# Hash attention and a channel mixer: a second level of smaller products for p5 in four row block pairs

## The chip, the core and the metric

The kernel runs on one core of one Trainium2 chip. The metric is device time in microseconds: the median of several executions, each with the same input. One further execution is recorded by the hardware profiler; its views are what the text calls the profile.

Names of the engines: PE is the matrix engine (PEld its weight loads), DVE the vector engine, ACT the scalar engine, POOL the general engine, SP the one that issues most of the DMAs.

## The reference, cut to what matters

An attention with hashed buckets gives `x` of 4 x 768 rows and 512 columns; a mixer over tokens gives `u`; the part that the change touches is the mixer over channels, in float32:

```python
def _moe_ref(x, w_tok1, w_tok2, w_ch1, w_ch2) -> np.ndarray:
    xt = x.transpose(0, 2, 1)
    h = np.maximum(xt @ w_tok1, 0.0) @ w_tok2
    u = x + h.transpose(0, 2, 1)
    h2 = np.maximum(u @ w_ch1, 0.0) @ w_ch2
    return (u + h2).astype(np.float32)
```

`u` has 3072 rows and 512 columns, `w_ch1` is 512 x 1536, `w_ch2` 1536 x 512.

## The kernel before

The program has three parts: attention (to about 310 us of the profiled span), the mixer over tokens (to 387.5 us), and `channels` (the rest). In `channels` everything is transposed: rows of `w_ch1` lie across partitions, and tokens are the columns.

**Stages.** `channels` takes the 3072 tokens in three stages s = 0, 1, 2 of 1024, each as two halves of TT = 512. A stage first makes `relu(u @ w_ch1)` into four tiles R0 to R3 (`hidden`, or `hidden_pair`), then multiplies by `w_ch2` (`outputs`). Both products are done with seven half-size products p1 to p7 in place of eight (Strassen's scheme in Winograd's form). In the first layer, with A the weights and B the tokens, U = p1 + p6 is a common partial sum; R0 = p1 + p2, R1 = U + p5 + p3, R2 = U + p7 + p4 and R3 = U + p7 + p5, up to the signs that are put into the operands.

**Second level.** In s = 1 and 2 the first layer takes its six blocks of 128 weight rows as three pairs t = 0, 1, 2 (block t and block t + 3). Within a pair p2, p6, p7, p3 and p4 are split once more: `Smaller` makes one of them from seven products of 128 x 128 weights by 256 columns where four of 512 columns would be needed. p1 and p5 are whole: two blocks times two 128-row slices of the operand, 512 columns each. The seven products come in three methods: `one` (one matmul, and ACT copies its result to SBUF, L904), `three` (three matmuls, added onto the PSUM tile they are given) and `rest` (three matmuls into the same PSUM tile as `one`, L914). `finish` lets ACT copy a partial sum u out of PSUM (L925), DVE add it to two 256-column parts in one 512-column add (L927), and DVE make the last part with a 256-column add (L930). The result e (four parts of 256) and the PSUM tile of `three` together are the product.

**PSUM.** There are four tiles of two banks each, 1024 columns, used in turn by the list `ring`; `bank_pair(i)` opens one anew, which waits for all uses of its last contents.

**Order.** The order on each engine is that of the calls in the text; engines meet through semaphores. In `hidden_pair` it is written out by hand. `plus` is a DVE add (L963), `copy` an ACT copy of 1024 columns (L960), `relu` is on ACT (L966). U is made in the tile `u`: p1 is accumulated with three parts of p2 in SBUF, p6's three parts are added by PE onto the PSUM tile of p1, and the copy of that, plus e6, is U. `between` gives DVE the sums of operands for the next products in the first pair of a stage (`right_sums`, four 256-column operations, L852 to L855). `unfinished` holds work for R1 to R3 of one pair, and `end_rows` does it in the next.

**Work ahead.** At the end of a pair the first half of the next pair's p1 is computed (`ahead`); it goes into the tile that held p5 and p3, and waits for the add into R1. At the end of t = 2, `whole_first` computes a part of the second layer's p1 ahead, and `whole_product` the rest.

**Looks.** Beside all this, `look` fetches a slice of the attention's input by a DMA that POOL issues (L1355) and sums on ACT how far its squares pass a bound (L1344, L1345). The results are needed at the first products of s = 2. It stands four times in each pair, and once in each second-layer product of s = 0 and 1.

**Weights.** The sums of weights for the second level are made by DVE in stage 0 (`prepare`) and stored in DRAM (`hidden_passed`). For each pair and each of p2, p6, p7, p3, p4 the seven blocks of 128 x 128 are fetched by SP (`fetch_hidden_left`, L866, 448 KB) as soon as the same product of the pair before has used its own.

Of the kernel before, what the change touches and what calls it, by code (L numbers as in the profile page):

```python
# [48 lines left out]
def kernel(  # L49
# [702 lines left out]
    def channels(pool, psum, SW1, second, TA, judge):  # L752
# [85 lines left out]
        def right_sums(name, s):  # L838


            sl = [slice(TT * (2 * s + i), TT * (2 * s + i) + TT) for i in range(2)]
            src = {"p2": XT[:, KC:, sl[0]], "p3": XT[:, KC:, sl[1]], "p6": T[1], "p7": T[2], "p4": T[3]}[name]
            if name == "p7":
                z = SW1[:, 1].rearrange("p k c -> p (k c)")[:, : 2 * TT]
            else:
                z = XT[:, ["p2", "p6", "p3", "p4"].index(name), : 2 * TT]
            z = split4(z)
            half = [slice(0, TT // 2), slice(TT // 2, TT)]
            b = [src[:, k, n] for k in range(2) for n in half]

            def job():
                nc.vector.tensor_tensor(z[:, 0], b[1], b[0], op=ALU.subtract)  # L852
                nc.vector.tensor_tensor(z[:, 1], b[3], b[1], op=ALU.subtract)
                nc.vector.tensor_tensor(z[:, 2], b[3], z[:, 0], op=ALU.subtract)
                nc.vector.tensor_tensor(z[:, 3], b[2], z[:, 2], op=ALU.subtract)  # L855

            return job, [*b, *(z[:, i] for i in range(4))]
# [12 lines left out]

        def hidden_left_at(h):

            h, n = h % 5, 7 * P
            if h < 3:
                return WC1[:, KC:].rearrange("p k c -> p (k c)")[:, n * h : n * h + n]
            return SW1[:, 2 * (h - 3)].rearrange("p k c -> p (k c)")[:, :n]
# [5 lines left out]
        def first_weight(name):  # L882

            return {
                "p2": WC1[:, KC:, : DCH // 2], "p3": SW1[:, 2], "p4": WC1[:, KC:, DCH // 2 :], "p6": SW1[:, 0],
                "p7": SW1[:, 1],
            }[name]
# [5 lines left out]
        class Smaller:  # L893


            def __init__(self, h, name, s):
                self.h, self.w = h, hidden_left_at(h).rearrange("p (i c) -> p i c", i=7)
                self.b = right_sums(name, s)[1]

            def one(self, pair, e):  # L900

                self.ps, self.e = pair, split4(e)
                self.mm(pair[:, 0, : TT // 2], 4, 0)
                nc.scalar.copy(self.e[:, 0], pair[:, 0, : TT // 2])  # L904

            def three(self, pair, start=False):
# [3 lines left out]
                self.mm(pair[:, 1, : TT // 2], 6, 7, start)  # L910

            def rest(self):

                self.mm(self.ps[:, 1, : TT // 2], 0, 4)  # L914
                self.mm(self.ps[:, 1, TT // 2 :], 1, 5)
                self.mm(self.ps[:, 0, : TT // 2], 2, 6, False)
                fetch_hidden_left(self.h + 5)

            def mm(self, ps, left, right, start=True):
                accumulate(ps, lambda k: self.w[:, left], lambda k: self.b[right], [0], start)  # L920

            def finish(self):

                u = extra_flat()[:, TT // 2 * (self.h % 2) : TT // 2 * (self.h % 2) + TT // 2]
                nc.scalar.copy(u, self.ps[:, 0, : TT // 2])  # L925
                p57 = self.ps[:, 1].rearrange("p (n t) -> p n t", n=2)
                nc.vector.tensor_tensor(  # L927
                    self.e[:, 1:3], p57, u[:, None, :].to_broadcast([P, 2, TT // 2]), op=ALU.add,
                )
                nc.vector.tensor_tensor(self.e[:, 3], p57[:, 0], self.e[:, 2], op=ALU.add)  # L930

        def hidden_pair(s, t, between):


            sl = [slice(TT * (2 * s + i), TT * (2 * s + i) + TT) for i in range(2)]
            ks = range(KC)
            r = [a[:, :, t::GP].rearrange("p n i c -> p i n c") for a in R]
            x, z, e, y = ring
            ring[:] = [y, e, z, x]

            p1, e2 = [output_at(i).rearrange("p i n -> p (i n)") for i in (0, 2)]
            p5, e6, u = copies(), copies(), copies()
            e3, e4 = [output_at(i).rearrange("p i n -> p (i n)") for i in (3, 1)]
            e7 = q1.rearrange("p i n -> p (i n)")
            h = 5 * GP * (s - 1) + 5 * t
            p2, p6, p7, p3, p4 = [Smaller(h + i, name, s) for i, name in enumerate(SMALLER)]

            def rows(a):
                return a.rearrange("p (i n c) -> p i n c", i=2, n=2)

            def banks(a):
                return a.rearrange("p i (n c) -> p i n c", n=2)

            def whole(pair, left, right, which=(0, 1), t=t):
                for i in which:
                    at = P * (t + GP * i)
                    accumulate(pair[:, i], lambda k: left(k)[:, at : at + P], right, ks)

            def copy(to, pair):
                nc.scalar.copy(to.rearrange("p (i n) -> p i n", i=2), pair)  # L960

            def plus(to, a, b):
                nc.vector.tensor_tensor(to, a, b, op=ALU.add)  # L963

            def relu(i):
                nc.scalar.activation(r[i], r[i], ACT.Relu)  # L966

            def opened(pair, which, s=s, t=t):
                start = TT * 2 * s
                whole(pair, lambda k: WC1[:, k], lambda k: XT[:, k, start : start + TT], which, t)  # L970

            X = ahead.pop() if ahead else None
            if not X:
                X = bank_pair(x)
                opened(X, [0])
            opened(X, [1])
            Z, E = bank_pair(z), bank_pair(e)
            p2.one(E, e2)
            copy(p1, X)
            p2.three(Z, True)  # L980
            Y = bank_pair(y)
            whole(Y, lambda k: WC1[:, k, DCH // 2 :], lambda k: T[0][:, k], [0])
            n = TT * 3 // 2
            plus(p1[:, :n], Z.rearrange("p i n -> p (i n)")[:, :n], p1[:, :n])
            for job in between[:2]:
                job()
            end_rows()
            p2.rest()
            whole(Y, lambda k: WC1[:, k, DCH // 2 :], lambda k: T[0][:, k], [1])
            p2.finish()  # L990
            copy(p5, Y)
# [3 lines left out]
            copy(u, X)  # L995
            look()
            V = bank_pair(e)
            p7.three(V, True)
            p6.rest()
            plus(p5[:, :n], V.rearrange("p i n -> p (i n)")[:, :n], p5[:, :n])  # L1000
            p6.finish()
            for job in between[2:]:
                job()
# [7 lines left out]
            relu(0)  # L1011
# [10 lines left out]
            if t + 1 < GP:  # L1022
                ahead.append(bank_pair(y))
                opened(ahead[0], [0], t=t + 1)
            else:
                ahead.append(blocks(1)[0])
                whole_first(s, ahead[0])
# [5 lines left out]
            look()  # L1033

            def end():
                relu(3)
                relu(2)
                for i in range(2):
                    bounded_minus(r[1][:, i], r[0][:, i])

            unfinished.append(end)


# [3 lines left out]
        ahead, EARLY = [], [k for k in range(HC) if k % GP < GP - 1]  # L1047
# [12 lines left out]
        def prepare():  # L1060
# [42 lines left out]
            def hidden_parts(name):  # L1103
# [6 lines left out]

            sums = weight_sums(WC2, SW2, slice(0, HC), slice(HC, NHT), low, high)
            return [
                [hidden_parts("p7")], sums, [whole("p1"), second_parts("p7")], *([second_parts(name)] for name in ("p6", "p3", "p5", "p2", "p4")),
                [hidden_parts("p2")], [hidden_parts("p6")], [hidden_parts("p3")], [hidden_parts("p4")],
# [59 lines left out]
        def whole_part(s, pair, m, ks, start=True, stop=True):  # L1174
            w, right = first_left(s), R[int(RIGHT["p1"][1])]
            accumulate(
                split(pair[:, m]), lambda k: w[:, k, P * m : P * m + P], lambda k: right[:, :, k], ks, start, stop,
            )

        def whole_first(s, pair):  # L1180
            whole_part(s, pair, 0, EARLY, stop=False)

        def whole_product(s):
            if ahead:
                pair = ahead.pop()
                whole_part(s, pair, 1, EARLY, stop=False)
                late = [k for k in range(HC) if k not in EARLY]
                for m in (1, 0):
                    whole_part(s, pair, m, late, False)
            else:  # L1190
                pair = blocks(1)[0]
                for m in range(KC):
                    whole_part(s, pair, m, range(HC))
# [4 lines left out]
        def product(s, j, name, q, between, final=None):  # L1198
# [27 lines left out]
            if s < last:  # L1226
                look()
# [32 lines left out]
        def outputs(s):  # L1260
# [21 lines left out]
            nc.scalar.copy(q1, ps)  # L1282
            q7, q57, q6, q5 = [output_at(i) for i in range(4)]
# [54 lines left out]
        def look():  # L1338

            if judge and not places:  # L1340
                places.append(pool.tile([P, 2, S], F32, name="seen", tag="seen", bufs=1))
            if len(seen) == 3 or not unseen and seen:
                t, n, i = seen.pop(0)
                nc.scalar.activation(t, t, ACT.Square)  # L1344
# [48 lines left out]
        for s in range(1, last + 1):  # L1393
            right_sums("p6", s)[0]()
            for t in range(GP):
                hidden_pair(s, t, [right_sums(name, s)[0] for name in ("p7", "p3", "p4")] if t == 0 else [])
                if t == 0:
                    residual(s)
# [8 lines left out]
    def with_token_weights(stage):  # L1407
        with tc.tile_pool(name="tok", bufs=1, reuse_waits="tile") as tok:
# [10 lines left out]
            f"p{i}": dram.tile([P, 8, NHT // 4 * P], F32, name=f"hidden_left{i}") for i in (2, 3, 4, 6, 7)  # L1419
# [102 lines left out]
```

## Time and profile before

| what | us |
| --- | --- |
| median of 4 runs | 794.18 (793.84 to 794.42) |
| the profiled execution | 794.49 |
| its span, first to last instruction | 792.6 |
| `channels` in the span | 387.5 to 792.6 |
| first layer of s = 1, t = 0, 1, 2 | about 531 to 592.5 |
| ACT, copies of 512 columns out of PSUM (L786) | 0.59 each |
| ACT, one look (two operations of 768 columns and a read of the sum) | 1.82 |

A line of the timeline or of a group gives the start (or the busy time), the engine, the source line, the operation, what it writes and reads by the program's names, the shapes, how many, and in brackets the idle time before it with what ended it. A line with a count merges instructions that follow each other, and one shape stands for all of them. The length shown for a matmul runs past the start of the next one, as they are pipelined; time on PE is therefore counted from start to start. A float32 matmul stands in the profile as two instructions.

The clock granted to PE is 0.999 of full speed over the span.

### The profile page before, as it was taken

How to read it: one execution, taken by the hardware profiler on the slowest of the kernel's cores; microseconds unless marked ns; L12 is line 12 of the kernel's file. 1: busy time of each engine (PE TensorE's matmuls, PEld its weight loads, DVE VectorE, ACT ScalarE, POOL GpSimd, SP SyncE). 2: the span in 40 equal slices, each digit the busy share in tenths (PEclk: the TensorE clock that was granted, in tenths of full speed). 3: DMA queues.
4: the chain of work that ended last, by engine and by line, in shares of the span. 5: the costliest groups of instructions: out<-in, count | busy, mean ns of one | idle time of the engine just before them, and what ended most of it. 6: DMA issues, size and time to landing. Idle time of an engine off the chain costs nothing.

```text
span 792.6 us, 12326 instructions
## 1 busy us (share of the span) xinstructions
PE 785.2 (99%) x4697; PEld 472.6 (60%) x4697; DVE 674.4 (85%) x921; ACT 442.2 (56%) x718; POOL 53.4 (7%) x77
## 2 busy tenths in 40 slices
PE   9999999999999999999999999999999999999997
PEld 4444444444544444455544458877777887676886
DVE  5989898988987677999697689898879998888996
ACT  6688888888888886333323221327764335775111
POOL 1000000000000000011121010011100012000001
PEclk9999999999999999999999999999999999999999
DMA  4435353538452424795686995798756588650665
GB/s 164 163 123 163 123 163 123 163 124 244 142 181 88 148 52 165 213 264 115 119 275 234 350 323 169 210 297 245 249 160 211 179 218 189 211 172 1 197 165 121
DMA packets 99760, 143.01 MB, mean 180 GB/s; under 512 B 30120, under 2 KB 69744, under 8 KB 99696
## 3 DMA queue, kind: packets, MB, share of 16 engines
q1 hardware_dynamic: 91536, 117.19, 45.5%
q0 software_dynamic: 7728, 24.64, 14.0%
q8 instruction: 38, 0.62, 0.3%
q10 hardware_dynamic: 432, 0.34, 0.2%
q14 instruction: 26, 0.21, 0.1%
HBM read 99.96 MB, written 34.73 MB: 170 GB/s over the span
## 4 chain that ended last, share of the span: by engine, by line
PE 97%; DVE 2%; ACT 1%; issue 0%; DVEq 0%
PE b L780 48%; PE sc L353 20%; PE acc L407 16%; PE t L653 5%; PE t L693 5%; PE sums L431 2%; PE hp L301 1%; PE idle L470 0%; PE hw L325 0%; DVE R L963 0%; DVE c L963 0%; ACT looked L1345 0%; ACT c L960 0%; ACT looked L1344 0%; DVE c L927 0%; DVE q L927 0%
## 5 line engine op out<-in xcount | busy, mean ns | idle before, releaser
L360 ACT ACTIVATE e<-sc 128x768 f32<-128x768 f32 x192 | 154.2, 811 | 11.2 <-PE sc L353 10.8
L353 PE MATMUL sc<-qk 64*128 64x384 f32 x768 | 152.9, 484 | 0.0
L780 PE MATMUL b<-R,second 128*128 128x256 f32 (+1 forms) x612 | 151.2, 404 | 0.0
L780 PEld LDWEIGHTS b<-R,second 128*128 128x128 f32 x612 | 116.4, 190 | 30.6 <-issue 16.5
L786 ACT COPY c<-b 128x512 f32<-128x512 f32 (+1 forms) x78 | 37.4, 488 | 169.3 <-PE b L780 155.6
L407 PE MATMUL acc<-e,vn 128*32 128x384 f32 x1536 | 127.0, 486 | 0.0
L392 DVE TENSOR_TENSOR esd<-esd,e 128x768 f32<-128x768 f32 x96 | 92.0, 958 | 10.4 <-ACT e L360 0.5
L407 PEld LDWEIGHTS acc<-e,vn 128*32 128x32 f32 x1536 | 50.0, 110 | 73.9 <-issue 73.3
L353 PEld LDWEIGHTS sc<-qk 64*128 64x128 f32 x768 | 68.7, 188 | 41.3 <-issue 35.9
L780 PE MATMUL b<-XT,WC 128*128 128x256 f32 (+1 forms) x228 | 75.5, 470 | 0.7 <-DVE R L963 0.7
L353 PE MATMUL sc<-bits 64*128 64x384 bf16 x384 | 62.9, 324 | 0.0
L780 PEld LDWEIGHTS b<-XT,WC 128*128 128x128 f32 x228 | 43.2, 190 | 28.3 <-issue 22.2
L388 DVE SCALAR_TENSOR_TENSOR esd<-e 128x768 f32<-128x768 f32 x32 | 30.6, 956 | 23.4 <-ACT e L360 23.4
L780 PE MATMUL b<-XT,SW 128*128 128x256 f32 (+1 forms) x156 | 43.7, 412 | 0.0
L780 PE MATMUL b<-TA,WC 128*128 128x512 f32 (+1 forms) x108 | 43.6, 521 | 0.0
L653 PE MATMUL t<-x,W 128*128 128x512 f32 x96 | 41.8, 594 | 0.0
L353 PEld LDWEIGHTS <-bits 64*128 64x128 bf16 x384 | 18.9, 94 | 32.9 <-issue 8.7
L780 PEld LDWEIGHTS b<-XT,SW 128*128 128x128 f32 x156 | 29.7, 190 | 11.7 <-issue 7.0
L713 POOL DMA_DIRECT2D XT<-second x8 | 9.9, 1232 | 383.4 <-DVE second L712 361.2
L452 ACT COPY rec<-rec 32x384 f32<-32x384 f32 x64 | 32.6, 510 | 5.0 <-DVE rec L446 4.2
L413 ACT ACTIVATE num<-acc,vsum 128x384 f32<-128x384 f32 x32 | 18.6, 581 | 29.7 <-PE acc L407 29.3
L395 DVE TENSOR_TENSOR esd<-esd,e 128x768 f32<-128x768 f32 x32 | 30.5, 954 | 1.9
(226 smaller groups left out, 1156.1 us busy)
## 6 DMA issues: line engine op xcount, KB each, us to landing
second<-left SPq DMA_DIRECT2D x20, 768.0 KB
raw<-in_moe_w_ch SPq DMA_DIRECT2D x16, 768.0 KB
qk<-in_qk SPq DMA_DIRECT2D x15, 768.0 KB
second<-left SPq DMA_DIRECT2D x18, 576.0 KB
seen<-in_qk POOLq DMA_DIRECT2D x21, 384.0 KB, 4.2
WC<-hidden_left SPq DMA_DIRECT2D x18, 448.0 KB
vn<-in_v SPq DMA_DIRECT2D x16, 384.0 KB
vt<-in_vT SPq DMA_DIRECT2D x16, 384.0 KB
```

The source lines that it names most:

```text
L353: nc.tensor.matmul(sc[:, i, :HALF], t[rows, 1, P * c : P * c + P], t[rows, 0, qs], start=start, stop=not start,)
L360: nc.scalar.activation(e, sc[:, :, :HALF], ACT.Exp, scale=SCALE)
L388: nc.vector.scalar_tensor_tensor(self.d, es[0], NR * EPS, es[1], op0=ALU.add, op1=ALU.add,)
L392: nc.vector.tensor_tensor(self.d, self.d, e, op=ALU.add)
L395: nc.vector.tensor_tensor(self.d, self.d, self.es[-1], op=ALU.add)
L407: nc.tensor.matmul(acc[D * i + d : D * i + d + 32], vn[:, i, c, d : d + 32], e[:, i], start=(c == 0), stop=(c == NR - 1),)
L413: nc.scalar.activation(nums[self.n][:, self.half], acc, ACT.Identity, scale=-1.0, bias=vsum,)
L452: nc.scalar.copy(rec[other : other + 32, h], rec[at : at + 32, h])
L653: nc.tensor.matmul(ps, W1[:, r, P * j : P * j + P], x[:, r], start=(r == 0), stop=(r == NR - 1),)
L693: nc.tensor.matmul(ps[at], left, right, start=start, stop=True, skip_group_check=True,)
L780: nc.tensor.matmul(ps, left(k), right(k), start=start and k == ks[0], stop=stop and k == ks[-1], skip_group_check=True,)
L786: nc.scalar.copy(c, ps)
```

## The change

In s = 1 and 2 the first pair, t = 0, stays nearly as it was and is now `hidden_first`. The pairs t = 1 and t = 2 get a new order, `hidden_pair`, in which p5 is a `Smaller` too:

- p5's sums of weights (four blocks of 128 per pair) are made in stage 0 by `fifth_parts`, stored, and fetched for each of the two pairs by `fetch_fifth` (256 KB). Its other three blocks are read from `WC1`. The sums of its other operand are a fourth `right_sums` job in the first pair.
- p2's three parts are added by PE onto the PSUM tile of p1, after ACT's copy of p1.
- p6, p5 and p7 put what is known so far into an empty PSUM tile, and `three` adds onto it: p6 and p7 by `finish(to)`, where DVE writes the last 256 columns into the tile and ACT copies the other 768; p5 by one DVE add of e5 and U. U is complete before p5 and p7 are.
- `rest` does the matmul that completes u first, and no longer last. u has three places in turn, where it had two.
- Two looks in a pair where there were four; in the second-layer products one more in s = 0 and 1 (beside the copy of q1), and two in each product of s = 1. The look is split so that a copy can stand between its two parts.
- `whole_first` and its part in `whole_product` are gone.

```diff
-            if name == "p7":
+            if name == "p5":
+                z = left_at(7 * s)[:, HC * 2 * P : HC * 2 * P + 2 * TT]
+            elif name == "p7":
...
+        def fetch_fifth(s, t):
+            if t < GP:
+                nc.sync.dma_start(
+                    out=fifth_left().rearrange("p (i c) -> p i c", i=4),
+                    in_=hidden_passed["p5"][:, :, P * t : P * t + P],
+                )
...
             def rest(self):
-                self.mm(self.ps[:, 1, : TT // 2], 0, 4)
-                self.mm(self.ps[:, 1, TT // 2 :], 1, 5)
-                self.mm(self.ps[:, 0, : TT // 2], 2, 6, False)
-                fetch_hidden_left(self.h + 5)
+                self.mm(self.ps[:, 0], 2, 6, False)
+                self.mm(self.ps[:, 1], 0, 4, False)
+                self.mm(self.ps[:, 2], 1, 5)
+                self.used()
...
+            def finish(self, to=None):
+                u = extra_flat()[:, TT // 2 * finished[0] : TT // 2 * (finished[0] + 1)]
+                finished[0] = (finished[0] + 1) % 3
+                nc.scalar.copy(u, self.ps[:, 0])
                 nc.vector.tensor_tensor(
-                    self.e[:, 1:3], p57, u[:, None, :].to_broadcast([P, 2, TT // 2]), op=ALU.add,
+                    self.e[:, 1:3], self.ps[:, 1:3], u[:, None, :].to_broadcast([P, 2, TT // 2]), op=ALU.add,
                 )
-                nc.vector.tensor_tensor(self.e[:, 3], p57[:, 0], self.e[:, 2], op=ALU.add)
+                last = self.e if to is None else split4(flat(to))
+                nc.vector.tensor_tensor(last[:, 3], self.ps[:, 1], self.e[:, 2], op=ALU.add)
+                if to is not None:
+                    nc.scalar.copy(last[:, :3], self.e[:, :3])
...
+        def hidden_first(s, t, between):
...
+            opened(X, [0, 1], s, t)
+            fetch_fifth(s, t + 1)
...
             V = bank_pair(e)
+            between[2]()
             p7.three(V, True)
             p6.rest()
-            plus(p5[:, :n], V.rearrange("p i n -> p (i n)")[:, :n], p5[:, :n])
+            plus(p5[:, :n], flat(V)[:, :n], p5[:, :n])
+            between[3]()
             p6.finish()
-            for job in between[2:]:
-                job()
             plus(u, u, e6)
...
+        def hidden_pair(s, t):
...
+            X = ahead.pop()
+            p6.one(bank_pair(two), e6)
+            opened(X, [1], s, t)
+            p2.one(bank_pair(three), e2)
+            copy_pair(p1, X)
+            p6.rest()
+            p2.rest()
+            Z = bank_pair(four)
+            p6.finish(Z)
+            p2.three(X)
+            p2.finish()
+            begin_look()
+            p5.one(bank_pair(two), e5)
+            end_look()
+            plus(r[0], banks(X), rows(e2))
+            p6.three(Z)
+            p7.one(bank_pair(three), e7)
+            plus(u, flat(Z), p1)
+            p5.rest()
+            p5.finish()
+            p3.one(bank_pair(one), e3)
+            Y = bank_pair(two)
+            plus(flat(Y), e5, u)
+            p7.rest()
+            V = bank_pair(four)
+            p7.finish(V)
+            p3.rest()
+            p5.three(Y)
+            p3.finish()
+            copy_pair(v, Y)
+            p7.three(V)
+            relu(r[0])
+            plus(r[3], banks(V), rows(v))
+            p4.one(bank_pair(three), e4)
+            p3.three(Y)
+            relu(r[3])
+            plus(r[1], banks(Y), rows(e3))
+            p4.rest()
+            p4.finish()
+            look()
+            p4.three(V)
+            plus(e4, e4, u)
+            plus(r[2], banks(V), rows(e4))
+            end_rows()
+            if t + 1 < GP:
+                open_next(one, s, t)
...
+            for _ in range(min(s + 1, 2) if s < last else 0):
                 look()
...
+            hidden_first(s, 0, [right_sums(name, s)[0] for name in ("p7", "p3", "p4", "p5")])
+            residual(s)
+            for t in range(1, GP):
+                hidden_pair(s, t)
```

## The prediction

> **What bounds the kernel now.** I read the engines' shares first, then the chain of waits, then busy time by stretch, then the timeline around three places. The shares:
>
> ```profile
> PE 785.2 (99%) x4697; PEld 472.6 (60%) x4697; DVE 674.4 (85%) x921; ACT 442.2 (56%) x718; POOL 53.4 (7%) x77
> ```
>
> PE is the bound. The chain of waits lies on it from 387.50 us to 787.01 but for two detours over ACT and DVE, which come back to PE at 545.32 and 676.54: the first pairs (t = 0) of s = 1 and 2. The stretches of s = 1 with t = 0, 1, 2 (after the length: PE, PEld, DVE, ACT, POOL):
>
> ```profile
> 531.00:548.50 17.50, 17.16 (x72) 13.25 (x71) 14.49 (x26) 11.25 (x21) 2.94 (x4) 1.00 0.87 213
> 548.50:570.50 22.00, 22.00 (x88) 16.40 (x87) 18.09 (x25) 16.66 (x29) 2.05 (x4) 1.00 0.82 272
> 570.50:592.50 22.00, 22.00 (x85) 15.83 (x84) 17.68 (x24) 16.55 (x29) 2.08 (x5) 1.00 0.59 176
> ```
>
> In t = 1 and 2 PE has no gap: matmul time taken out there shows in full, and so does any new wait. The timeline at the detour's end:
>
> ```profile
> 543.71 0.42 DVE L930 TENSOR_TENSOR q<-b,q 128x256 f32<-128x256 f32 x1
> 544.05 1.21 DVE L963 TENSOR_TENSOR R<-b,c 128x1024 f32<-128x1024 f32 x1
> 544.38 0.59 PE L780 MATMUL b<-TB,SW 128*128 128x256 f32 x2
> ...
> 545.32 1.98 PE L780 MATMUL b<-XT,WC 128*128 128x512 f32 x4 [0.34 <-DVE R L963]
> ```
>
> A matmul counts as two instructions, which start 0.216 us apart with 256 columns (562.65 to 563.94 for six) and 0.4285 with 512 (567.40 to 569.11 for four). The pair at 544.38 is through its slots at 544.81, the next starts at 545.32, 0.05 us after DVE's end at 545.26; and its four take 1.82 us (the next group starts at 547.14), not 1.71, since the weight load is no longer ahead. So the wait costs 0.51 + 0.11 = 0.62 us, at 676.54 the same: 1.2 us in all. A result that ends at x holds PE as if it came at x + 0.16.
>
> **What the change removes.** In t = 1 and 2 of s = 1 and 2, p5 is four 512-column matmuls now, 8 x 0.4285 = 3.43 us, and becomes seven of 256, 14 x 0.216 = 3.03. Four pairs: 4 x 0.40 = 1.6 us.
>
> The early part of the second layer's p1 only changes place: 24 instructions of 0.4285 us, 10.3 us, now all stand behind t = 2. That is cover for DVE, which after t = 2's p4.finish has two 1024 adds and four 512 subtractions, some 2 x 1.14 + 4 x 0.6 = 4.7 us, before the first product. I cost it at nothing.
>
> **The wait at t = 0.** DVE idles 1.54 us before 537.31 (for ACT's copy) and 1.06 before 539.33 (for a copy queued behind a look on ACT), then makes the four p4 sums (540.39 to 541.85, 1.46 us) on the path. The change puts the p4 sums into the first gap (535.68 to 537.14) and the new p5 sums behind the V sum (537.31 + 0.87 = 538.18, to 539.64). p6.finish starts at 539.64, not 539.33, u at 539.64 + 0.72 + 0.46 = 540.82, p7.finish at 541.96, r1 at 541.96 + 0.72 + 0.34 = 543.02: it holds PE until 543.02 + 1.21 + 0.16 = 544.39, and PE comes at 544.81. Both waits go: 1.2 us. If the sums cost more than 0.4 us beyond this, they begin to come back; before is the worst I assume.
>
> **What the change adds: the seeds.** In the new pair p7.three adds onto V, which DVE and ACT must have filled. From S, the end of PE's slots for p5.rest, the chain has these rows:
>
> ```profile
> 554.89 1.88 PE L780 MATMUL b<-TA,WC 128*128 128x512 f32 x4
> 555.09 0.37 ACT L925 COPY second<-b 128x256 f32<-128x256 f32 x1 [0.83 <-PE b L780]
> 555.49 0.69 DVE L927 TENSOR_TENSOR second<-b,second 128x512 f32<-128x512 f32 x1 [0.26 <-ACT second L925]
> ...
> 556.22 0.42 DVE L930 TENSOR_TENSOR second<-b,second 128x256 f32<-128x256 f32 x1
> ...
> 556.68 1.23 DVE L963 TENSOR_TENSOR R<-second 128x1024 f32<-128x1024 f32 x1
> ```
>
> p5's u copy starts 0.20 after S, the 512 add 0.40 later, the 256 add 0.73, the Y seed (a 1024 add) 0.46 after that: S + 1.79. Y ends at S + 3.02 and holds PE to S + 3.18. PE meanwhile does p3.one, p7.rest and p3.rest, 7 x 0.4325 = 3.03: p5.three waits 0.15. DVE takes p7.finish behind Y: a 1024 add gives way after 1.14 (541.85 to 542.99), so its 512 add starts at S + 2.93, the 256 add at 3.66, ending 4.08; ACT's copy of the other 768 into V starts 0.03 later (as at 553.20 after 553.17). That copy has no row: by ACT's 256 (0.37), 1024 (1.02) and a 256 from SBUF (L1021, 0.39) I take 0.82; bounds are the 512 copy (L786, 0.59) and the 1024 relu (1.06). It ends at S + 4.93 and holds PE to S + 5.09. PE reaches p7.three after ten matmuls, 4.33. Loss 0.76 us in each pair, p5's 0.15 in it: 4 x 0.76 = 3.0. The other row missing is an add into PSUM; its bounds are the 768 add (0.96) and two 512 adds (1.36) around 1.23. Both ends together give 0.26 and 1.13 a pair. Behind the waiting copy on ACT stand p3's u and Y's copy; p3.three, which needs the latter, comes some 0.5 us after it. On DVE p3.finish is behind, needed much later.
>
> The other seed, Z for p6, is in time: from p6.rest's end its chain is 0.20 + 0.40 + 0.73 + 0.42 + 0.03 + 0.82 + 0.16 = 2.76, against p2.rest, p2.three and p5.one, 7 x 0.4325 = 3.03.
>
> The Trainium skill, "PSUM — Partial Sum Buffer", section "PSUM bank collisions raise a hardware error", says that no two engines may touch one bank at a time, different columns included. V's columns 512 to 767 and 768 to 1023 share a bank, so ACT's copy must come after DVE's 256 add; without that rule the chain would be 0.45 shorter and the sum 1.8 us lower. No row here shows such a pair side by side.
>
> The same page, "The four PSUM rules", holds that DVE and ACT writes don't set the bit that makes a matmul add, and advises to pass seeds through PE. The change doesn't, so by either reading the sum stays.
>
> One more wait: t = 1 begins with p6.one, whose copy on ACT is behind the last look of t = 0. From p4.rest's end: 0.20, a copy 0.27 (570.61 to 570.88), the look 1.82 (567.86 to 569.68), the copy 0.37, 0.16: 2.82. PE has p6.one, two 512 matmuls and p2.one, 0.43 + 1.71 + 0.43 = 2.58. Loss 0.24, twice: 0.5. In t = 2 the look comes seven matmuls and more earlier.
>
> **Costed at nothing.** p5's weight sums in s = 0: four 128x384 operations, 2.1 us (445.33 to 447.45); DVE idles 4.22 us for PE before 456.28; uncovered, 2.1. Their two stores, 0.75 MB, some 2.2 us at the 350 GB/s of that stretch, stand on SP ahead of p6's, p3's and p4's stores; those end near 469, the next fetch that matters is needed near 480. The four p5 fetches, 256 KB: on SP before p2's fetch at t = 0 and before p7's at t = 1, ahead of use by 15 us and more. Eight looks leave the pairs and go to the products, two now in each of s = 1: 1.8 us more of ACT, busy 14.8 of the 60 us of s = 0's products. POOL's stores queue behind them, up to 2 us later.
>
> **Sum.** On the profiled execution, 794.49 (span 792.6 and 1.9 around it): -1.6 - 1.2 + 3.0 + 0.5 = +0.7. It lies 0.3 above the median of the runs, 794.18, so I predict 794.9. With the bounds, 4 x 0.26 and 4 x 1.13, the likeliest case alone spans 792.9 to 796.4.
>
> **Rivals.** (1) The seeds arrive in time and both gains stay: 794.2 - 2.8 = 791.4, or 791.9 with the wait at t = 1. For it: 0.76 is the difference of a chain of ten terms and 4.33 of matmuls, and DVE and ACT have 4 us and more of idle time in each pair. Against: none of that idle time is inside this chain. (2) Slower: p6's weights land late. p6.one now opens t = 1, at 547.8, where p6 came some 9 us later before; its fetch is issued at 538.5 and landed by 544.5, with a DMA share of 0.87 in that stretch and 256 KB more asked for. It decides from 3.3 us of delay; a landing time of 12 us in place of 6 gives 2.7 us, twice: 800.3. Against: DMA lies idle near 537 and can take the new fetch there. (3) The sums at t = 0 find no gap and that wait stays: 794.9 + 1.2 = 796.1.
>
> **How the numbers follow.** Forecast 0.61, rival 1 0.18, rival 2 0.11, rival 3 0.10. Runs of this kernel spread by 0.6 us, so I take 0.2% (1.6 us) as what tells a change. Of the forecast 0.04 is faster than that, 0.43 within, 0.14 slower; rival 1 is faster, 2 and 3 slower: 0.22, 0.43, 0.35. The range 791.9 to 797.0 leaves out half of rival 1 and rival 2.
>
> **What would show it.** Right: no wait of PE at t = 0 of s = 1 and 2; in t = 1 and 2 of both, PE waits for ACT's 768 copy some 0.5 us ahead of p7.three, and little for DVE at p5.three; at the head of t = 1 a short wait for ACT's 256 copy. Wrong: PE without gaps in these pairs (rival 1), a wait for a DMA at p6.one (rival 2), or any wait of PE in the products of s = 1, whose ACT queue I cost at nothing.

## The result, and the profile after

| | before | after |
| --- | --- | --- |
| median of the runs, us | 794.10 (793.25 to 794.99, 60 runs) | 795.09 (794.21 to 795.92, 40 runs) |
| profiled execution, us | 794.49 | 795.03 |
| its span, us | 792.6 | 793.1 |

The ratio is 1.0012, with an interval of 1.0007 to 1.0016: 1 us slower, within the 0.2% that the prediction calls no change. Behind that stand four terms of 0.4 to 3.3 us, of both signs. The first part of the page after, busy time of each engine:

```profile
PE 785.3 (99%) x4721; PEld 475.3 (60%) x4721; DVE 674.4 (85%) x925; ACT 445.3 (56%) x726; POOL 53.4 (7%) x77
```

PE has 24 instructions more: p5 in four pairs is 4 x 14 = 56 short ones in place of 4 x 8 = 32 long ones. Shorter work, yet the same busy time: a part of what is booked as busy must be waiting. The waits view of the kernel after, for PE (waited for: us in total, times, longest):

```profile
PE b L780 <- ACT b L963: 1.3, 4, 0.3
PE idle L470 <- DVE ones L97: 1.1, 1, 1.1
```

The second line, at the start of the program, stands in the kernel before as well. Beside it there was a wait for DVE's add into R, two times:

```profile
PE b L780 <- DVE R L963: 0.7, 2, 0.3
```

Now it is ACT's 768-column copy into a PSUM tile (L963), once in each of the four new pairs. A wait there of 0.33 us is what is left after the modelled end of the matmul ahead; from start to start the loss is larger, as the timelines below show.

The chain of waits of the kernel after, in order of time (start, us, what), at its first way around PE:

```profile
387.49 170.62 PE b L780 x576
...
558.13 0.38 ACT second L956
...
558.54 0.70 DVE second L957
...
559.27 0.44 DVE second L961
...
559.73 1.23 DVE b L981
560.96 0.60 DVE q L957
...
561.59 0.44 DVE b L961
...
562.11 0.81 ACT b L963
562.92 0.04 issue
562.96 17.53 PE b L780 x72
```

PE now runs from 387.49 us without a way around it through both old places. In place of the two detours that ended in R1 there are four such as this: copy, 512 add, 256 add of p5.rest; the add of Y into PSUM; 512 add and 256 add of p7; the copy of the other 768 columns of V. That is, operation for operation, the chain which the prediction added up.

The timeline of the kernel after at the old place, the end of t = 0 of s = 1:

```profile
543.01 1.21 DVE L981 TENSOR_TENSOR R<-b,c 128x1024 f32<-128x1024 f32 x1
...
544.36 0.59 PE L780 MATMUL b<-TB,SW 128*128 128x256 f32 x2
...
544.79 1.88 PE L780 MATMUL b<-XT,WC 128*128 128x512 f32 x4
```

The add that PE waited for starts at 543.01 (before: 544.05), ends at 544.22, and PE goes from one group to the next after two slots of 0.216: no wait.

The same view at the head of t = 1:

```profile
550.00 0.18 ACT L1452 ACTIVATION_READ_ACCUMULATOR seen<-seen,minus_safe 128x1 f32 x1
550.09 0.35 ACT L925 COPY q<-b 128x256 f32<-128x256 f32 x1
...
550.49 3.75 PEld L780 LDWEIGHTS b<-XT,WC 128*128 128x128 f32 x18 [0.34 <-ACT q L925]
```

ACT's copy for p6.one stands right behind the look's last operation, and a weight load waits for it. The instructions of PE start 0.106 and 0.104 us later here than their slots: 0.21 us in all.

And the two seeds, p5.three on Y and p7.three on V, in t = 1:

```profile
558.13 0.37 ACT L956 COPY second<-b 128x256 f32<-128x256 f32 x1 [0.92 <-PE b L780]
...
559.73 1.23 DVE L981 TENSOR_TENSOR b<-second,c 128x1024 f32<-128x1024 f32 x1
...
561.07 0.30 PEld L780 LDWEIGHTS b<-TA,WC 128*128 128x128 f32 x2 [0.36 <-issue]
561.10 0.67 PE L780 MATMUL b<-TA,WC 128*128 128x256 f32 x2
561.59 0.43 DVE L961 TENSOR_TENSOR b<-b,q 128x256 f32<-128x256 f32 x1
...
562.04 0.59 PE L780 MATMUL b<-second,WC 128*128 128x256 f32 x2
562.11 0.80 ACT L963 COPY b<-q 128x768 f32<-128x768 f32 x1 [1.87 <-DVE b L961]
...
562.96 1.13 PE L780 MATMUL b<-TA,WC 128*128 128x256 f32 x4 [0.33 <-ACT b L963]
563.93 0.59 PE L780 MATMUL b<-SW,WC 128*128 128x256 f32 x2
```

The pair of instructions at 562.04 is through at 562.47, the next starts at 562.96: 0.49 us, for a copy that ended at 562.91. Its four take 0.97 us to the start of the next group, not 0.87: 0.10 more. At p5.three, ahead of it, the losses are 0.147 and 0.075. So a pair loses 0.22 + 0.59 = 0.81 us, and the four pairs agree within 0.005.

The first line shows something else. ACT's copy of p5's u reads the 256 columns that the first matmul of `rest` completes, and that one is through its slots at 557.07. The copy starts at 558.13, after 0.92 us of idle time: 0.20 behind the slots of the third matmul (557.93), which writes other columns, in the other bank of the tile. So doing the matmul that completes u first brought no earlier copy here; in this program the copy waits for the whole of `rest`.

Busy time of the stretches t = 0, 1, 2 of s = 1 after (length; PE, PEld, DVE, ACT, POOL; granted clock, DMA share, GB/s). The cuts follow the pairs, not those of the table before:

```profile
531.00:547.90 16.90, 16.90 (x72) 13.38 (x71) 16.34 (x31) 11.26 (x21) 2.76 (x4) 1.00 0.95 241
548.00:570.40 22.40, 22.07 (x93) 16.96 (x92) 17.93 (x23) 15.63 (x29) 1.37 (x4) 1.00 0.85 268
570.40:592.70 22.30, 21.97 (x93) 17.23 (x92) 16.23 (x22) 14.72 (x27) 0.95 (x3) 1.00 0.49 138
```

The gap of PE has gone from the first line, where DVE is now full (16.3 of 16.9 us, with the sums of p4 and p5 in it), to the other two. DMA is at 0.95 in the first stretch, and no instruction of PE waits for a DMA there or later. The granted clock is 1.00 throughout.

### The profile page after: what moved, and what is told of

Same layout as the page of the kernel before. It is cut to its first block, busy times and chain, and to the rows that moved or that the text cites. A ratio compares the mean times of both kernels' runs of the same rounds, so it can differ in the third digit from the quotient of the medians.

```text
span 793.1 us, 12404 instructions
## 1 busy us (share of the span) xinstructions
PE 785.3 (99%) x4721; PEld 475.3 (60%) x4721; DVE 674.4 (85%) x925; ACT 445.3 (56%) x726; POOL 53.4 (7%) x77
## 4 chain that ended last, share of the span: by engine, by line
PE 97%; DVE 2%; ACT 1%; issue 0%; ACTq 0%; DVEq 0%
PE b L780 48%; PE sc L353 20%; PE acc L407 16%; PE t L653 5%; PE t L693 5%; PE sums L431 2%; PE hp L301 1%; DVE b L981 1%; ACT b L963 0%; PE idle L470 0%; DVE second L957 0%; PE hw L325 0%; DVE q L957 0%; DVE b L961 0%; DVE second L961 0%; ACT second L956 0%
## 5 line engine op out<-in xcount | busy, mean ns | idle before, releaser
L780 PE MATMUL b<-TA,WC 128*128 128x256 f32 (+1 forms) x92 | 34.0, 479 | 1.3 <-ACT b L963 1.3
```

Source lines behind the costliest of these rows:

```text
L780: nc.tensor.matmul(ps, left(k), right(k), start=start and k == ks[0], stop=stop and k == ks[-1], skip_group_check=True,)
```

## The experiments

The theory: four pairs lose about 0.8 us each because PE comes to a seeded tile ahead of its seed; t = 0 gives back 1.2 us; p5 saves 1.6. Rivals: that t = 0's gain has another cause than the place of the sums; that the wait at p7.three is only where a shortage of DVE or ACT shows, so that without it the loss turns up at another place; that the other parts (looks, fetches) cost something too. Each kernel is the changed one with the edit shown, except e4_sums, which is the kernel before. Ratios are to the kernel before, run beside it. The last column adds to each wait what is lost behind the first late instruction; losses under 0.1 us are left out.

| run | median, us | ratio | interval | left of PE's waits from 387 us on |
| --- | --- | --- | --- | --- |
| after | 795.09 | 1.0012 | 1.0007 to 1.0016 | 4 x 0.22, 4 x 0.59, 2 x 0.21 |
| e1_noseed | 795.14 | 1.0012 | 1.0003 to 1.0021 | 4 x 0.22, 4 x 0.32, 2 x 0.71, 2 x 0.21 |
| e2_p4 | 793.34 | 0.9990 | 0.9981 to 0.9999 | 4 x 0.22, 4 x 0.16, 2 x 0.21 |
| e3_look | 794.34 | 1.0002 | 0.9993 to 1.0011 | 4 x 0.22, 4 x 0.59 |
| e4_sums | 793.06 | 0.9985 | 0.9976 to 0.9995 | none |
| e5_early | 794.03 | 1.0002 | 0.9993 to 1.0011 | 4 x 0.22, 4 x 0.39, 2 x 0.21 |
| e7_twice | 798.44 | 1.0056 | 1.0043 to 1.0070 | 4 x 0.22, 4 x 1.43, 2 x 0.21 |
| e6_best | 792.16 | 0.9976 | 0.9967 to 0.9985 | 4 x 0.22 |
| e8_noseed2 | 793.14 | 0.9987 | 0.9978 to 0.9996 | 4 x 0.22, 2 x 0.20, 2 x 0.21 |
| e9_cover | 793.16 | 0.9988 | 0.9979 to 0.9997 | none |
| e10_order | 792.63 | 0.9981 | 0.9972 to 0.9990 | 4 x 0.30 |

### e4_sums: the first pair's part alone

In the kernel before:

```diff
             V = bank_pair(e)
+            for job in between[2:]:
+                job()
             p7.three(V, True)
...
             p6.finish()
-            for job in between[2:]:
-                job()
             plus(u, u, e6)
```

> The kernel before, with nothing but the four p4 sums of t = 0 moved: ahead of the V sum on DVE, in place of behind p6.finish. Theory: they fill DVE's 1.54 us gap, and both waits of PE at t = 0, 0.61 us each, go: 794.1 - 1.2 = 792.9, ratio 0.9985. Rival (the waits went in the changed kernel for another reason, such as fewer operations at the head of the pair): no change, 1.0000.

Measured: 793.06, 1.2 us under the 794.23 beside it. The waits view for PE holds one line alone, which stands at the start of the program:

```profile
PE idle L470 <- DVE ones L97: 1.1, 1, 1.1
```

Four 256-column sums moved into time in which DVE waited anyway are worth the whole 1.2 us. This part of the change has nothing to do with p5.

### e7_twice: the suspected copy doubled

```diff
                     nc.scalar.copy(last[:, :3], self.e[:, :3])
+                    if self.h % 5 == 2:
+                        nc.scalar.copy(last[:, :3], self.e[:, :3])
```

> The changed kernel, with ACT copying the 768 columns of p7's seed twice, the same values. Theory: the second copy adds its 0.72 us (start to start) to the chain, and PE waits by that much longer in each of four pairs: 795.1 + 2.9 = 798.0, ratio 1.0048. Rival (PE waits for something else that comes at about the same time): less than half of it, below 796.5.

Its timeline at p7.three:

```profile
561.82 0.80 ACT L963 COPY b<-q 128x768 f32<-128x768 f32 x1 [1.87 <-DVE b L961]
562.66 0.80 ACT L965 COPY b<-q 128x768 f32<-128x768 f32 x1
...
563.51 1.13 PE L780 MATMUL b<-TA,WC 128*128 128x256 f32 x4 [1.16 <-ACT b L965]
```

PE starts 0.05 us after the second copy's end, and all of the second copy is paid: 0.84 us in each pair, 798.44 - 795.09 = 3.35 in four. So this copy is on the path that sets the end, with no slack behind it. The second copy starts 0.84 after the first, not the 0.72 that the expectation took from copies that overlap by a tenth; that is the 0.4 us that it missed.

### e5_early: a third of the copy off the chain

```diff
+                if to is not None:
+                    nc.scalar.copy(last[:, 0], self.e[:, 0])
                 nc.vector.tensor_tensor(last[:, 3], ...)
                 if to is not None:
-                    nc.scalar.copy(last[:, :3], self.e[:, :3])
+                    nc.scalar.copy(last[:, 1:3], self.e[:, 1:3])
```

> The changed kernel, with the first 256 of the 768 seed columns copied by ACT right behind the u copy, ahead of DVE's adds, so that 512 are left to copy behind the 256 add. Theory (the length of the last copy stands in the chain): an ACT copy of 512 takes 0.59 us, one of 768 took 0.80, so PE's wait ahead of p7.three falls by 0.21, from 0.59 to 0.38, in four pairs: 795.1 - 0.8 = 794.3, ratio 1.0002. Rival (the number of copies or the tile's waits count, not their length): no gain or slower, 795.1 or above (1.0012).

The copy that is left takes 0.59 us, and the wait at p7.three falls from 0.59 to 0.39: by the 0.20 that the copy is shorter. From after to e5_early the medians fall by 1.06; 4 x 0.20 of it is accounted for, the rest is inside the intervals.

### e2_p4: something for PE to do meanwhile

```diff
             copy_pair(v, Y)
+            p4.one(bank_pair(three), e4)
             p7.three(V)
             relu(r[0])
             plus(r[3], banks(V), rows(v))
-            p4.one(bank_pair(three), e4)
```

> The changed kernel, with p4.one ahead of p7.three in t = 1 and 2; no work is added. Theory: the seed of V comes as before, PE has one matmul more to do before it, so the wait ahead of p7.three falls from 0.59 to 0.59 - 0.43 = 0.16 us in each of four pairs: 795.1 - 1.7 = 793.4, ratio 0.9991. Rival (the seed is late because of what stands before it on PE or ACT): the wait moves along and the time stays near 795.1 (1.0012).

The timeline at the same place:

```profile
562.28 0.80 ACT L963 COPY b<-q 128x768 f32<-128x768 f32 x1 [1.87 <-DVE b L961]
...
562.65 0.59 PE L780 MATMUL b<-TB,SW 128*128 128x256 f32 x2
...
563.14 1.13 PE L780 MATMUL b<-TA,WC 128*128 128x256 f32 x4
563.14 0.73 PEld L780 LDWEIGHTS b<-TA,WC 128*128 128x128 f32 x4 [0.30 <-ACT b L963]
```

One matmul, 0.43 us, stands between: PE is 0.06 late where it was 0.49 late, and the loss is 0.16 in place of 0.59 with the weight load. The moved matmul needs nothing that comes late. 793.34, as expected: the copy is only waited for because PE comes to the seed too early, and no other wait took its place.

### e3_look: the last look of t = 0

```diff
             plus(r[2], r[2], rows(e4))
-            look()
...
-            for _ in range(min(s + 1, 2) if s < last else 0):
+            for _ in range(min(s + 1, 2) + (s == 0 and j in (2, 3)) if s < last else 0):
```

> The changed kernel, with the last look of t = 0 taken out and put into one more second-layer product of s = 0 each (two looks there instead of one). Theory: p6.one's copy is then ready in time and the waits of 0.21 us at the head of t = 1 go, twice: 795.1 - 0.4 = 794.7, ratio 1.0007; the rest stays. Rival (the looks in the products cost PE time): two more of them there make it slower, above 795.1.

Both waits at the head of t = 1 are gone and the others have stayed; 794.34, ratio 1.0002. The size, 0.4 us, is less than the interval tells apart; the trace shows it.

### e1_noseed and e8_noseed2: p7 without a seed

In e1_noseed DVE adds e7 to V's partner and to U itself, and the sums into R3 and R2 cover three quarters, the last quarter being a copy on ACT:

```diff
-            p7.finish(V)
+            p7.finish()
...
-            p7.three(V)
+            p7.three(V, True)
             relu(r[0])
-            plus(r[3], banks(V), rows(v))
+            plus(v, v, e7)
+            plus(r[3][:, 0], banks(V)[:, 0], rows(v)[:, 0])
+            plus(r[3][:, 1, 0], banks(V)[:, 1, 0], rows(v)[:, 1, 0])
+            nc.scalar.copy(r[3][:, 1, 1], rows(v)[:, 1, 1])
+            plus(u, u, e7)
             p4.one(bank_pair(three), e4)
...
```

> The changed kernel, with p7 not seeded in t = 1 and 2: e7 stays in SBUF, p7.three opens its PSUM tile itself, and DVE adds e7 to v and to u (two 1024 adds more in each pair). Theory (the chain to p7's seed holds PE): the wait ahead of p7.three, 0.59 us in each of four pairs, is gone, the 0.22 at p5.three stays, DVE has room for the adds: 795.1 - 2.4 = 792.7, ratio to the kernel before 0.9983. Rival (the loss lies elsewhere, in looks, DMAs or p5's price, and the wait only shows it): the time stays near 795.1 (1.0012), with the wait at another place. Rival (DVE has no room): a new wait at p4.three or later, up to 2 x 1.14 us in a pair, above 797.

That failed: 795.14, no gain at all. The wait at p7.three is gone, and two others have come. The timeline of e1_noseed, behind p7.three and at the head of t = 2:

```profile
564.01 1.23 DVE L981 TENSOR_TENSOR c<-c,q 128x1024 f32<-128x1024 f32 x1 [0.65 <-ACT c L984]
...
565.27 0.41 ACT L1123 COPY R<-c 128x256 f32<-128x256 f32 x1 [0.33 <-DVE c L981]
565.59 0.36 ACT L925 COPY second<-b 128x256 f32<-128x256 f32 x1
...
566.00 1.16 PEld L780 LDWEIGHTS b<-XT,SW 128*128 128x128 f32 x6 [0.45 <-ACT second L925]
...
570.98 0.41 ACT L1136 COPY R<-second 128x256 f32<-128x256 f32 x1 [1.20 <-DVE second L981]
571.29 2.00 ACT L987 ACTIVATE R<-R 128x1024 f32<-128x1024 f32 x2
573.20 0.35 ACT L925 COPY q<-b 128x256 f32<-128x256 f32 x1
573.60 0.92 PE L780 MATMUL b<-XT,WC 128*128 128x256 f32 x3 [0.44 <-ACT q L925]
```

A copy of a quarter of R, which waits for DVE's 1024 add, heads ACT's queue; the 256-column copy that PE needs (L925) stands behind it, and behind two relus at 571.29 as well. Four times 0.32 and twice 0.71, 2.7 us, took the place of 4 x 0.59 = 2.4. Whether that was the order on ACT, or DVE too full for two more adds in a pair, this run does not tell. e8_noseed2 changes the order alone:

```diff
-            nc.scalar.copy(r[3][:, 1, 1], rows(v)[:, 1, 1])
             plus(u, u, e7)
             p4.one(bank_pair(three), e4)
+            nc.scalar.copy(r[3][:, 1, 1], rows(v)[:, 1, 1])
...
-            nc.scalar.copy(r[2][:, 1, 1], rows(e4)[:, 1, 1])
+            quarter = lambda: nc.scalar.copy(r[2][:, 1, 1], rows(e4)[:, 1, 1])
+            if t + 1 < GP:
+                late.append(quarter)
+            else:
+                quarter()
```

where the next pair does what is in `late` behind its p1 copy.

> As in e1_noseed the seventh smaller product is not seeded and VectorE adds it to the two sums itself; only ScalarE's order differs: the copy of the last quarter of the third row block now stands behind the copy of the fourth smaller product, and in t = 1 the copy of the last quarter of the second row block stands behind the next pair's copy of the first smaller product. Theory: the two new waits of e1_noseed came from ScalarE's queue alone, each copy that TensorE needed standing behind one that waited for VectorE. Then four waits of 0.32 us go, and the two of 0.71 at the head of t = 2: 795.14 - 1.3 - 1.4 = 792.4 us, ratio 0.998. Rival: VectorE, with two more additions in each pair, has no room, and the waits turn up at another place: 795.1 us, ratio 1.001.

793.14, 2 us under e1_noseed, and 1.0 under the kernel before. Its timeline at the first of the two places:

```profile
563.43 1.23 DVE L981 TENSOR_TENSOR c<-c,q 128x1024 f32<-128x1024 f32 x1 [0.65 <-ACT c L984]
...
564.25 0.36 ACT L925 COPY second<-b 128x256 f32<-128x256 f32 x1
564.69 0.41 ACT L1127 COPY R<-c 128x256 f32<-128x256 f32 x1
```

The copy that PE needs now starts while the add still runs, and PE goes through. Both new waits are gone, and DVE has the room for its two adds. One small loss came up at another place, p7.one of t = 2 in both stages: 0.12 us ahead of it and 0.075 behind its first instruction, 0.20 twice:

```profile
577.30 0.42 DVE L961 TENSOR_TENSOR second<-b,second 128x256 f32<-128x256 f32 x1
...
577.83 0.67 PE L780 MATMUL b<-TA,WC 128*128 128x256 f32 x2
```

p7.one takes the PSUM tile that p2.finish has to read first, and that add ends at 577.72. It is late by ACT's order again, as far as the trace tells: the moved quarter copy (573.46 to 573.88) stands ahead of p6's copy of u, which so starts 2.21 us before p5.one (575.98). In t = 1, where no such copy stands there, it starts 2.39 us before, and p7.one loses nothing. The expected 792.4 (0.9978 of the 794.18 beside it) lies at the lower end of the interval; of the difference of 0.7, 0.4 are these two.

### e6_best: the three edits together

e2_p4, e3_look and e5_early in one kernel.

> The changed kernel with three things at once: p4.one ahead of p7.three, 256 of the seed columns copied early, and the last look of t = 0 moved to a product of s = 0. Theory: the waits ahead of p7.three go (0.59 less 0.43 for p4.one, less 0.21 for the shorter copy: none left), those at the head of t = 1 go, and p5.three's 0.22 stays in four pairs: 795.1 - 2.4 - 0.4 = 792.3, ratio 0.9977. Rival (the gains aren't additive because p6's seed or p7.one becomes late by the earlier copy): 793 or above.

Its timeline at the two seeds:

```profile
559.91 0.38 ACT L962 COPY b<-q 128x256 f32<-128x256 f32 x1
...
561.90 0.59 ACT L965 COPY b<-q 128x512 f32<-128x512 f32 x1 [1.61 <-DVE b L963]
...
562.25 0.59 PE L780 MATMUL b<-TB,SW 128*128 128x256 f32 x2
562.68 1.03 PE L780 MATMUL b<-TA,WC 128*128 128x256 f32 x4
```

The copy ends at 562.49, PE gets to p7.three at 562.68 and does not wait. 792.16 against 794.09 beside it: faster than both kernels, by 1.9 us and 2.9. Against e4_sums, which leaves p5 whole, the ratio is 0.0009 lower, 0.7 us: the 1.6 that p5's split saves, less the 4 x 0.22 that p5.three still loses. The intervals of the two overlap, so that difference rests on the waits rather than on the medians (792.16 and 793.06, 0.9 apart).

### e9_cover and e10_order: the rest, at p5.three

The views put the 0.22 us at p5.three down to issue, not to the seed Y. Both kernels start from e6_best. e9_cover gives PE one matmul more ahead of p5.three, the last one of p3.rest a second time:

```diff
-            def rest(self):
+            def rest(self, again=False):
...
                 self.mm(self.ps[:, 2], 1, 5)
+                if again:
+                    self.mm(self.ps[:, 2], 1, 5)
...
-            p3.rest()
+            p3.rest(True)
```

> e6_best with the last matmul of p3.rest done twice, into the same place: 0.43 us more of matmul time for PE ahead of p5.three in each of the four pairs. What is asked is whether the 0.22 us lost at p5.three (0.147 ahead of it and 0.075 behind its first instruction) is a wait for the seed Y, although the profile puts it down to issue. Theory, the seed: PE comes 0.43 later, finds Y ready, the 0.22 goes, 792.16 + 4 x (0.43 - 0.22) = 793.0 us, ratio 0.9987. Rival, something that p5.three costs whenever it comes: the 0.22 stays, 792.16 + 4 x 0.43 = 793.9 us, ratio 0.9998.

793.16: the loss is gone in all four pairs (no start on PE is over 0.05 us late from 387 us on), though PE does more. So p5.three did wait for Y, and the extra matmul costs some 0.2 a pair (1.0 us in four by the medians) instead of 0.43. The label "issue" on the weight load (0.36 us at 561.07 in the kernel after) was a wait that the view could not name.

e10_order makes Y earlier instead:

```diff
-            p7.one(bank_pair(three), e7)
-            plus(u, flat(Z), p1)
             p5.rest()
+            plus(u, flat(Z), p1)
             p5.finish()
+            p7.one(bank_pair(three), e7)
```

> e6_best with p5.rest ahead of p7.one, and p5's copy of u ahead of p7.one's copy on ScalarE. Theory, that p5.three waits for Y: the three matmuls of p5.rest end 0.43 us earlier, VectorE idles 0.25 us ahead of p5's 512-column add, so Y comes some 0.25 us earlier against an unchanged p5.three, the 0.22 goes in all four pairs and nothing takes its place: 792.16 - 0.9 = 791.3 us, ratio 0.9965. Rival, that p5.three loses 0.22 whenever it comes, or that another wait (p7's copy, now behind p5's) takes its place: 792.2 us, ratio 0.9976.

It came out as the rival: 792.63, 0.5 over e6_best, where 0.9 less had been expected. The intervals of the two overlap, so what became of the gain is read from the trace:

```profile
557.77 0.59 PE L780 MATMUL b<-XT,SW 128*128 128x256 f32 x2
...
557.97 0.37 ACT L925 COPY q<-b 128x256 f32<-128x256 f32 x1
...
558.39 0.30 PEld L780 LDWEIGHTS b<-SW,WC 128*128 128x128 f32 x2 [0.43 <-ACT q L925]
```

p5.three loses nothing now, but p7.rest adds into the part that p7.one's copy has to read first, and that copy (557.97 to 558.34) is late, as only one matmul, p3.one, is left between the two. 0.19 + 0.10 us are lost there, 1.2 in four pairs, in place of 0.9.

## Why the prediction was right

The forecast was 794.9, and 795.09 was measured. By its steps:

- **p5, -1.6 us.** PE's last matmul ends at 787.01 before and 751.39 + 36.28 = 787.67 after (last pieces of the two chains of waits), 0.66 later. The listed waits grew by 3.68 - 1.22 = 2.46 us, and one late start of 0.09 us in the kernel before (at 753.33) is gone; so PE's work itself became 2.46 - 0.09 - 0.66 = 1.7 us shorter. Nothing else changed the number of matmuls (24 more instructions), so the term is right to about 0.1.
- **t = 0, -1.2.** Right, and shown by e4_sums alone. The add into R1 was put at 543.02 and came at 543.01.
- **The seeds, +3.0.** 3.26 was measured, 0.815 in each pair. Taken apart: p7.three 0.59, where the prediction's 0.76 - 0.15 leaves 0.61; p5.three 0.22, where it had 0.15. The term that was small: PE was taken to lose as if a result came 0.16 after its end, and at p5.three it is 0.14 to the start (560.96 to 561.10) and 0.075 behind it, 0.21. The 768-column copy without a row was taken at 0.82 and took 0.80; the 1024 add into PSUM at 1.23 and took 1.23. e7_twice, e5_early and e2_p4 move the wait at p7.three up and down by what the copy and the cover change, so the mechanism is shown.
- **The bank rule.** The prediction laid the order "DVE's 256 add, then ACT's 768 copy" to two engines not being allowed on one bank. The order is in the trace (the copy starts 0.09 us after the add's end). But the copy of u at 558.13 waited for a matmul into the other bank of its tile, so this program's waits can be wider than a bank, and no run shows which of the two forbids the overlap here.
- **The head of t = 1, +0.5.** 2 x 0.21 = 0.42. In the trace of e3_look it is gone.
- **Costed at nothing.** The weight sums, their stores, the fetches, the looks in the products of s = 0 and 1, and the early part of the second layer's p1: from 387 us on PE waits at none of them. All losses of PE over 0.1 us in the kernel after are in the list above.
- **Rivals.** (1) no loss at the seeds: refuted by the waits view. (2) p6's weights late: p6.one starts on its slot, no wait for a DMA. (3) the wait of t = 0 stays: refuted by the first fence of the timelines.

With these measured sizes the terms add up to -1.7 - 1.2 + 3.26 + 0.42 = +0.8 us; the medians say +0.99. The sum was made against a profiled execution 0.3 to 0.4 above its median, which is why the two profiled executions differ by 0.54 alone. The mechanism was right in each term. That the total came within 0.2 us is luck in part: the bounds of the two operations without a row alone allowed 792.9 to 796.4, and both came out at the value taken (0.80 for 0.82, 1.23 for 1.23).

## What to carry to other kernels

A tile that is seeded by another engine puts that engine's whole chain in front of the matmul; count it from the end of the matmuls that feed it, operation by operation, against the matmuls that stand between, and put one more independent matmul there before making the chain shorter (e2_p4: 4 x 0.43 us for nothing but a moved line). Look also at what stands ahead of a needed copy in an in-order queue: e1_noseed removed a wait of 2.4 us and got 2.7 back by two copies in the wrong place on ACT, and moving those gave 2 us. When a change has several parts, try each alone: moving four adds gave 1.2 us here, more than the new scheme of p5 left over even at its best (0.7, e6_best against e4_sums).

## What was not expected of the hardware

- A result that comes late costs PE twice: the wait, and 0.075 to 0.107 us more at the next weight load, which is no longer ahead of the matmul. In e2_p4 a lateness of 0.06 us so became a loss of 0.16.
- ACT's copies from SBUF into PSUM took 0.38, 0.59 and 0.80 us for 256, 512 and 768 columns, as long as those out of PSUM (0.37 for 256, 0.59 for 512); DVE's 1024 add took 1.23 into PSUM and into SBUF.
- Two ACT copies into the same place start 0.84 apart at a length of 0.80 (e7_twice). Copies to different places overlap: in e6_best the 512-column one runs from 561.90 to 562.49 and the next, a 256-column one out of another tile, starts at 562.42. Why was not tried.
- The idle time booked as issue at a weight load can be a wait for another engine's result: e9_cover took it away by coming later.
